# V of a batch in few large loads: pairing attention heads as (i, i+4)

## The chip, the cores and the metric

One core of a Trainium2 chip runs the whole program. The metric is the device time of one execution, in microseconds (us). Engines are written PE (TensorE), DVE (VectorE), ACT (ScalarE), POOL (GpSimd) and SP (SyncE); SPq and POOLq are the instruction queues of SP and POOL in which DMAs are issued.

## What is computed

The reference has two stages. The first is chunked attention over q, k, v of shape (4 batches, 8 heads, 768 positions, 64): each chunk of 32 queries looks at its own keys, 16 keys to the left, 8 to the right, and 8 memory keys of its head.

```python
for c in range(S // 32):
    l_start, r_end = max(0, 32 * c - 16), min(S, 32 * c + 32 + 8)
    k_full = concat(mem_k, k[:, :, l_start:r_end])      # v_full likewise
    scores = q[:, :, 32 * c:32 * c + 32] @ k_full.T / sqrt(64)
    out[:, :, 32 * c:32 * c + 32] = softmax(scores) @ v_full
```

The second stage treats the result as x of shape (4, 768, 512): a dot product with `w_gate` scores each position, the 128 best positions of each batch go through relu(xe @ w1) @ w2, weighted by the sigmoid of their score, and are added to x.

## The kernel before

The work goes by pairs of heads: 16 pairs n, four (pr = 0 to 3) for each batch b. Heads 2*pr and 2*pr+1 form a pair; one lies on partitions 0 to 63 and the other on 64 to 127. The 768 positions of a head are cut into 8 windows (NG) of 96 queries, three chunks each, and a window needs 120 keys.

V lies in one of two buffers (`vbufs`, float32, one for even and one for odd batches) with 128 partitions: 64 for each head of a pair, in four groups of 16 (15 rows of two keys each, and one row of memory values in the 16th). A window reaches 16 keys ahead of its queries, so window 0 begins before the sequence and window 7 ends after it. `load_v` therefore has three sorts of loads for each head and group: windows 1 to 6 (line 91, one load for each pair), window 0 without its first two rows (line 93), and window 7 without its last row (line 95). A fourth sort (line 98) brings the memory values. All are issued on SP. The rows that no load writes are set to zero once, at the start (lines 123 and 124).

`load_qk` issues q and k on POOL (line 81) with a cast to float16. For batch 0 the order is pair 0, pair 1, pairs 2 and 3.

In the loop over n (line 481) an iteration runs, in the order of every engine's program: the scores of pair n+1, first half (PE line 250, exponentials on ACT line 255, called `es`); the transposes of k of pair n+2 (PE line 203, copied by DVE line 220 to `kw`, memory keys filled in by POOL line 227); the values of pair n, first half (PE line 276); `cast_v(n+2)` (ACT line 234, V to float16 in `vc`, one of four slots); the scores' second half; the transposes of q of pair n+3 (ACT line 211 copies them to `qT`); the values' second half; `normalise` (DVE lines 283 and 284, writes x of the batch). Before the loop stand the transposes of pairs 0 and 1, `cast_v(0)`, the scores of pair 0, and `cast_v(1)`.

The second stage of batch b-1 is spread over the iterations of batch b as `hook` steps: dot products (DVE, tile `junk`, line 319), rows (PE 329), comparisons (DVE 353), counts, selection, gather (PE 390), two layers (PE 415 and 424), and a scattered addition into the output (POOL, line 428). `m_store` (SP, lines 305 and 306) writes x of batch b-1 to the output at the start of batch b; the scattered addition waits for that store, and the next store for the addition. The loads of batch b+2 are issued in the iteration with pr == 2 of batch b. After the loop the last batch's second stage runs alone.

The order on each engine is the order in which the program is written (a manual schedule): nothing is moved by a planner, and an instruction that waits holds up all that stand behind it on its engine.

Of the kernel before, what the change touches and what calls it, by code (L numbers as in the profile page):

```python
# [8 lines left out]
FP = mybir.dt.float32  # L9
# [17 lines left out]
def kernel(  # L27
# [13 lines left out]
    nc = tc.nc  # L41
# [37 lines left out]
    def load_qk(b, src, dst, p0, n):  # L79
        h0 = 2 * p0  # L80
        nc.gpsimd.dma_start(out=dst[:, h0:h0 + 2 * n, :],
                            in_=_dap(src, (b * H + h0) * HD, [[512, 96], [HD, 2 * n], [1, 512]]))

    def load_v(b, p0, n):
        t = vbufs[b % 2]
        for h in range(2):
            for jj in range(4):
                o = 64 * h + 16 * jj
                base = (b * H + 2 * p0 + h) * HD + 2 * jj * D
                for i in range(n):  # L90
                    nc.sync.dma_start(out=t[o:o + 15, p0 + i, 1:7, :],  # L91
                                      in_=_dap(v, base + 2 * i * HD + 80 * D, [[8 * D, 15], [96 * D, 6], [1, 128]]))
                nc.sync.dma_start(out=t[o + 2:o + 15, p0:p0 + n, 0, :],  # L93
                                  in_=_dap(v, base, [[8 * D, 13], [2 * HD, n], [1, 128]]))
                nc.sync.dma_start(out=t[o:o + 14, p0:p0 + n, 7, :],  # L95
                                  in_=_dap(v, base + 656 * D, [[8 * D, 14], [2 * HD, n], [1, 128]]))
            for i in range(n):
                nc.sync.dma_start(out=t[64 * h + 15:64 * h + 64:16, p0 + i, :, :],  # L98
                                  in_=_dap(mem_v, (b * H + 2 * (p0 + i) + h) * n_mem * D,
                                           [[2 * D, 4], [0, NG], [1, 128]]))  # L100
# [3 lines left out]
    load_qk(0, q, q16s[0], 0, 1)  # L104
    load_qk(0, k, k16s[0], 0, 1)
# [8 lines left out]
    for p0, n in ((1, 1), (2, 2)):  # L114
        load_qk(0, q, q16s[0], p0, n)
        load_qk(0, k, k16s[0], p0, n)
# [5 lines left out]
    for t in vbufs:  # L122
        nc.vector.memset(t[:, :, 0, :], 0.0)
        nc.vector.memset(t[:, :, 7, :], 0.0)
    for p0 in range(NP):
        load_v(0, p0, 1)
# [19 lines left out]
    ones8 = cst.tile([128, NG], F16, tag="ones8")  # L146
# [12 lines left out]
    def mem_keys():  # L159
        p_mk = pmm.tile([128, NPR, n_mem], F16, tag="pm", name="p_mk")  # L160
        for pr in range(NPR):
            nc.tensor.transpose(out=p_mk[:, pr, :], in_=memk16[:, 2 * pr:2 * pr + 2, :],
                                identity=ident16[0:n_mem, 0:n_mem])
        nc.vector.tensor_copy(out=memkT, in_=p_mk.rearrange("p n (j s) -> p n s j", s=2))
# [149 lines left out]
    def m_dot(b, bls, c0=0, c1=Dm, dst=None):  # L314
        m, x = mods[b], xs[b]
        dst = m.scr if dst is None else dst
        for bl in bls:
            junk = mod.tile([128, Dm], FP, tag="junk", name="junk")
            nc.vector.scalar_tensor_tensor(out=junk[:, c0:c1], in0=x[:, bl, c0:c1], scalar=1.0, in1=wgb[:, c0:c1],  # L319
                                           op0=ALU.mult, op1=ALU.mult, accum_out=dst[:, bl:bl + 1])  # L320

    def m_x16(b, lo, hi, c0=0, c1=Dm):
        nc.vector.tensor_copy(out=mods[b].x16[:, lo:hi, c0:c1], in_=xs[b][:, lo:hi, c0:c1])  # L323
# [157 lines left out]
    for n in range(NPR):  # L481
# [24 lines left out]
        if pr == 2 and b + 2 < B:  # L506
            alloc_batch(b + 2)
            for p0 in (0, 2):
                load_qk(b + 2, q, q16s[b + 2], p0, 2)
                load_qk(b + 2, k, k16s[b + 2], p0, 2)  # L510
                load_v(b + 2, p0, 2)
# [9 lines left out]
    m_dot(b, range(NB), 384, 512, scrB)  # L521
# [6 lines left out]
    m_x16(b, 0, NB, 384, 512)  # L528
# [42 lines left out]
```

## Time and profile before

| | us |
|---|---|
| three runs, median (lowest to highest) | 244.46 (241.13 to 245.14) |
| profiled execution, time | 242.47 |
| profiled execution, span of its instructions | 240.8 |

The span runs from the first instruction to the last; the profiled execution's own time is 1.67 us longer. Busy time within the span was 119.7 us on PE, 83.8 us on DVE, 75.3 us on ACT and 30.7 us on POOL.

### The profile page before, as it was taken

The page shows a single profiled execution, that of the slowest core. Times are in us where ns is not written, and L with a number is a line of the kernel's source. Part 1 is how long each engine was busy: PE and PEld are TensorE (multiplying, and loading weights), DVE is VectorE, ACT ScalarE, POOL GpSimd, SP SyncE. Part 2 cuts the span into 40 slices and gives each one's busy share as a digit, 9 for nine tenths or more (in the row PEclk, how much of TensorE's full clock was granted, in tenths as well). Part 3 has the DMA queues.
Part 4 walks back from the last instruction along what each step waited for, and adds up shares of the span by engine and source line. Part 5 has one row for each costly group of instructions (what it writes and reads, how often), then busy time and mean ns, then how long its engine had stood idle before and what let it go on. Part 6 is the DMA issues. An engine that isn't in the chain of part 4 may idle for free.

```text
span 240.8 us, 5533 instructions
## 1 busy us (share of the span) xinstructions
PE 119.7 (50%) x2264; PEld 98.8 (41%) x2264; DVE 83.8 (35%) x255; ACT 75.3 (31%) x152; POOL 30.7 (13%) x55
## 2 busy tenths in 40 slices
PE   0360801025260079179609920997950478574670
PEld 0350701025250068168608710887740367453540
DVE  6110110011120019348201634673370497548410
ACT  0123203060600282383046450727615252001010
POOL 7254000000050001002200003000000300002011
PEclk9999999999999999999955975557985556677587
DMA  6979994111379222221992275422218380004703
GB/s 93 167 118 206 212 209 87 44 43 44 97 124 209 71 63 58 60 57 54 174 177 55 62 210 130 98 56 72 56 49 264 45 241 26 0 3 87 218 0 44
DMA packets 32681, 24.58 MB, mean 102 GB/s; under 512 B 5264, under 2 KB 28432, under 8 KB 32656
## 3 DMA queue, kind: packets, MB, share of 16 engines
q0 software_dynamic: 9104, 9.47, 25.4%
q1 hardware_dynamic: 23552, 14.76, 22.7%
q8 instruction: 17, 0.28, 0.5%
q14 instruction: 8, 0.07, 0.1%
HBM read 25.30 MB, written 7.34 MB: 136 GB/s over the span
## 4 chain that ended last, share of the span: by engine, by line
SPq 39%; DMA 28%; DVE 10%; PE 9%; issue 9%; ACT 2%; POOL 1%; POOLq 1%; DVEq 0%; ACTq 0%
DMA v<-in_v_dram 22%; SPq L91 16%; SPq L95 9%; SPq L93 8%; SPq L98 6%; DMA out_dram<-x 6%; DVE junk L319 3%; PE p_m L415 3%; DVE gr L353 2%; PE p_x L276 2%; PE p_m L424 2%; ACT es L255 1%; PE p_s L250 1%; PE p_t L203 1%; DVE x L284 1%
## 5 line engine op out<-in xcount | busy, mean ns | idle before, releaser
L255 ACT ACTIVATE es<-p_s,maskb 128x256 f16<-128x256 f32 x96 | 38.6, 479 | 28.0 <-PE p_s L250 28.0
L250 PE MATMUL p_s<-qT,kw 64*64 64x96 f16 x512 | 24.7, 262 | 39.3 <-POOL kw L227 22.2
L234 ACT CAST vc<-v 128x1024 f16<-128x1024 f32 x16 | 16.9, 1056 | 86.7 <-DMA v<-in_v_dram 65.3
L220 DVE COPY kw<-p_t 128x512 f16<-128x512 f16 x32 | 12.1, 419 | 74.9 <-PE p_t L203 74.9
L250 PEld LDWEIGHTS <-kw 64*64 64x64 f16 x512 | 19.6, 148 | 43.3 <-POOL kw L227 22.6
L276 PE MATMUL p_x<-vc,es 64*96 64x65 f16 (+1 forms) x768 | 33.4, 242 | 0.0
L203 PE MATMUL p_t<-ident,k 96*64 96x96 f16 x256 | 12.7, 267 | 35.3 <-ACT qT L211 35.3
L276 PEld LDWEIGHTS <-es 64*96 64x96 f16 (+1 forms) x768 | 26.5, 142 | 5.2 <-issue 0.6
L203 PEld LDWEIGHTS <-k 96*64 96x64 f16 x256 | 10.5, 152 | 37.1 <-issue 36.3
L227 POOL COPY kw<-memkT 128x64 f16<-128x64 f16 x16 | 9.0, 564 | 128.0 <-DVE kw L220 88.5
L284 DVE TENSOR_TENSOR x<-p_x,rd 128x768 f32<-128x768 f32 x16 | 15.3, 958 | 14.6 <-DMA out_dram<-x 14.1
L428 POOL DMA_INDIRECT out_dram<-y,idx x4 | 6.7, 1682 | 75.2 <-DMA out_dram<-x 36.7
L319 DVE SCALAR_TENSOR_TENSOR junk<-x,wgb 128x512 f32<-128x512 f32 (+2 forms) x30 | 15.8, 581 | 0.1
L211 ACT COPY qT<-p_t 128x768 f16<-128x768 f16 x16 | 12.9, 809 | 2.7 <-PE p_t L203 2.7
L353 DVE TENSOR_SCALAR gr<-brow,scr 128x768 f16<-128x768 f32 x24 | 13.4, 617 | 0.1
L203 PE MATMUL p_t<-ident,q 96*64 96x96 f16 x256 | 12.3, 263 | 1.9 <-DVE kw L220 1.8
L283 DVE RECIPROCAL rd<-p_x 128x12 f32<-128x12 f32 x16 | 3.7, 230 | 26.5 <-PE p_x L276 26.5
L415 PEld LDWEIGHTS <-w_sb 128*128 128x128 f16 x128 | 10.4, 123 | 3.9 <-DVE gate L405 3.0
L203 PEld LDWEIGHTS <-q 96*64 96x64 f16 x256 | 10.1, 149 | 3.4 <-issue 2.1
L415 PE MATMUL p_m<-xeT,w_sb 128*128 128x128 f16 x96 | 8.9, 265 | 2.9 <-DVE gate L405 2.9
L390 PEld LDWEIGHTS <-x 128*128 128x128 f16 x96 | 9.3, 138 | 1.3 <-DVE sel L382 0.7
L323 DVE CAST x<-x 128x1024 f16<-128x1024 f32 (+2 forms) x11 | 8.4, 783 | 0.0
(89 smaller groups left out, 101.8 us busy)
## 6 DMA issues: line engine op xcount, KB each, us to landing
v<-in_v_dram SPq DMA_DIRECT2D x128, 45.0 KB
out_dram<-x SPq DMA_DIRECT2D x4, 1152.0 KB
q<-in_q_dram POOLq DMA_DIRECT2D x7, 384.0 KB, 7.2
k<-in_k_dram POOLq DMA_DIRECT2D x7, 384.0 KB, 8.6
w_sb<-in_moe_w_dram POOLq DMA_DIRECT2D x2, 1024.0 KB, 16.0
out_dram<-x SPq DMA_DIRECT2D x4, 384.0 KB
v<-in_v_dram SPq DMA_DIRECT2D x48, 13.0 KB
v<-in_v_dram SPq DMA_DIRECT2D x48, 14.0 KB
```

The lines of the kernel that those rows point to most:

```text
L91: nc.sync.dma_start(out=t[o:o + 15, p0 + i, 1:7, :], in_=_dap(v, base + 2 * i * HD + 80 * D, [[8 * D, 15], [96 * D, 6], [1, 128]]))
L93: nc.sync.dma_start(out=t[o + 2:o + 15, p0:p0 + n, 0, :], in_=_dap(v, base, [[8 * D, 13], [2 * HD, n], [1, 128]]))
L95: nc.sync.dma_start(out=t[o:o + 14, p0:p0 + n, 7, :], in_=_dap(v, base + 656 * D, [[8 * D, 14], [2 * HD, n], [1, 128]]))
L203: nc.tensor.transpose(out=p_t[64 * h:64 * h + 64, j, 2:98], in_=src[b][:, 2 * pr + h, 64 * j:64 * j + 64], identity=ident16[0:96, 0:96])
L234: nc.scalar.copy(out=vcs[n % SLOTS][:, :, :, 0:64], in_=vbufs[b % 2][:, pr, :, :].rearrange("p g (s d) -> p g s d", d=D))
L250: nc.tensor.matmul(out=p_s[o:o + 64, s, 96 * gi:96 * gi + 96], lhsT=kw[o:o + 64, g, s, :], rhs=qf[o:o + 64, 96 * g:96 * g + 96], start=Tru ...
L255: nc.scalar.activation(out=es[:, :, :, 32 * c:32 * c + 32], in_=pv[:, :, :, 32 * c:32 * c + 32], func=AF.Exp, bias=maskb[:, c:c + 1], scal ...
L276: nc.tensor.matmul(out=p_x[r0:r1, h, c0:c0 + 65], lhsT=es[o:o + 64, s, gi, q0:q1], rhs=vc[o:o + 64, GROUPS[half][gi], s, :], start=(s == 0 ...
L284: nc.vector.tensor_tensor(out=xs[b][:, :, 128 * pr:128 * pr + 128].rearrange("p g (h d) -> p h g d", d=D), in0=pv[:, :, :, 0:64], in1=rd.t ...
L319: nc.vector.scalar_tensor_tensor(out=junk[:, c0:c1], in0=x[:, bl, c0:c1], scalar=1.0, in1=wgb[:, c0:c1], op0=ALU.mult, op1=ALU.mult, accum ...
L353: nc.vector.tensor_scalar(out=m.gr[:, bl, :], in0=m.brow, scalar1=m.scr[:, bl:bl + 1], scalar2=None, op0=ALU.is_lt)
L415: nc.tensor.matmul(out=p_h[:, 0, 128 * fi:128 * fi + 128], lhsT=w1_sb[:, dch, f0:f0 + 128], rhs=m.xeT[:, dch, :], start=(dch == 0), stop=( ...
```

## The change

Pairs are now (i, i+4). The lower half of the partitions holds heads 0 to 3 of a batch and the upper half heads 4 to 7. Since a head's 768 positions are exactly eight windows of 96, window 0 of head h+1 stands 96 positions after window 7 of head h, and one load with a step of 96 positions covers all 32 windows of four heads on 15 partitions. A batch then has 8 such loads and 8 of memory values. Windows 0 and 7 now also bring keys of the neighbouring head; `cast_v` multiplies these two windows by a column of zeros and ones (`ones8`) on DVE, while ACT casts windows 1 to 6. Only the very first and the very last head of V, whose neighbour lies outside the tensor, keep separate loads (four each). Batch 0 is loaded as pair 0 and then pairs 1 to 3; the upper half of pair 0 is issued on ACT.

q and k follow: batch 0 loads heads 0 and 4 together, then heads 1 to 3 and 5 to 7 (q, k, q, k); later batches load heads 0 to 3 and 4 to 7. The output columns of `normalise`, the partial dot products and the partial float16 copy for the last batch take the new order of heads.

```diff
-    def load_v(b, p0, n):
-        t = vbufs[b % 2]
-        for h in range(2):
+    def load_v(b, p0, n, engines=(nc.sync, nc.sync)):
+        t = vbufs[b % 2].rearrange("p n g d -> p (n g) d")
+        for hh in range(2):
+            eng = engines[hh]
+            h = 4 * hh + p0
+            lo = 1 if (b, h) == (0, 0) else 0
+            hi = NG * n - 1 if (b, h + n) == (B - 1, H) else NG * n
             for jj in range(4):
-                o = 64 * h + 16 * jj
-                base = (b * H + 2 * p0 + h) * HD + 2 * jj * D
-                for i in range(n):
-                    nc.sync.dma_start(out=t[o:o + 15, p0 + i, 1:7, :],
-                                      in_=_dap(v, base + 2 * i * HD + 80 * D, [[8 * D, 15], [96 * D, 6], [1, 128]]))
-                nc.sync.dma_start(out=t[o + 2:o + 15, p0:p0 + n, 0, :], ...
-                nc.sync.dma_start(out=t[o:o + 14, p0:p0 + n, 7, :], ...
+                o = 64 * hh + 16 * jj
+                base = (b * H + h) * HD + (2 * jj - 16) * D
+                u = NG * p0
+                eng.dma_start(out=t[o:o + 15, u + lo:u + hi, :],
+                              in_=_dap(v, base + 96 * D * lo, [[8 * D, 15], [96 * D, hi - lo], [1, 128]]))
+                if lo:
+                    eng.dma_start(out=t[o + 2:o + 15, u, :], in_=_dap(v, base + 16 * D, [[8 * D, 13], [1, 128]]))
+                if hi < NG * n:
+                    eng.dma_start(out=t[o:o + 14, u + hi, :], in_=_dap(v, base + 96 * D * hi, [[8 * D, 14], [1, 128]]))
             for i in range(n):
-                nc.sync.dma_start(out=t[64 * h + 15:64 * h + 64:16, p0 + i, :, :], ...
+                eng.dma_start(out=t[64 * hh + 15:64 * hh + 64:16, NG * (p0 + i):NG * (p0 + i + 1), :],
+                              in_=_dap(mem_v, (b * H + h + i) * n_mem * D, [[2 * D, 4], [0, NG], [1, 128]]))
...
-    load_qk(0, q, q16s[0], 0, 1)
-    load_qk(0, k, k16s[0], 0, 1)
+    load_qk(0, q, q16s[0], 0, 2, 4)
+    load_qk(0, k, k16s[0], 0, 2, 4)
...
-    for p0, n in ((1, 1), (2, 2)):
-        load_qk(0, q, q16s[0], p0, n)
-        load_qk(0, k, k16s[0], p0, n)
+    for h0 in (1, 5):
+        load_qk(0, q, q16s[0], h0, 3)
+        load_qk(0, k, k16s[0], h0, 3)
...
-    for p0 in range(NP):
-        load_v(0, p0, 1)
+    load_v(0, 0, 1, (nc.sync, nc.scalar))
+    load_v(0, 1, 3)
...
         for pr in range(NPR):
-            nc.tensor.transpose(out=p_mk[:, pr, :], in_=memk16[:, 2 * pr:2 * pr + 2, :], ...
+            b, i = divmod(pr, NP)
+            for hh in range(2):
+                nc.tensor.transpose(out=p_mk[64 * hh:64 * hh + 64, pr, :], in_=memk16[:, b * H + 4 * hh + i, :], ...
...
-        nc.scalar.copy(out=vcs[n % SLOTS][:, :, :, 0:64],
-                       in_=vbufs[b % 2][:, pr, :, :].rearrange("p g (s d) -> p g s d", d=D))
+        vc, vt = vcs[n % SLOTS], vbufs[b % 2]
+        nc.scalar.copy(out=vc[:, 1:7, :, 0:64], in_=vt[:, pr, 1:7, :].rearrange("p g (s d) -> p g s d", d=D))
+        for g in (0, NG - 1):
+            nc.vector.tensor_scalar(out=vc[:, g, :, 0:64], in0=vt[:, pr, g, :].rearrange("p (s d) -> p s d", d=D),
+                                    scalar1=ones8[:, g:g + 1], scalar2=None, op0=ALU.mult)
...
-    for p0 in (0, 2):
-        load_qk(1, q, q16s[1], p0, 2)
-        load_qk(1, k, k16s[1], p0, 2)
-        load_v(1, p0, 2)
+    for h0 in (0, 4):
+        load_qk(1, q, q16s[1], h0, 4)
+        load_qk(1, k, k16s[1], h0, 4)
+    load_v(1, 0, NP)
```

The loads of batches 2 and 3 change like those of batch 1. Of the four memsets on the V buffers two small ones are left.

## Rows read from the trace of the kernel before

**Rows 1.** The page's first part: span and number of instructions.

```profile
span 240.8 us, 5533 instructions
```

**Rows 2.** The page's fourth part: chain that ended last, by engine, then line.

```profile
SPq 39%; DMA 28%; DVE 10%; PE 9%; issue 9%; ACT 2%; POOL 1%; POOLq 1%; DVEq 0%; ACTq 0%
```

**Rows 3.** Waits over the span: us in total, times, longest.

```profile
POOL out_dram L428 <- DMA out_dram<-x: 36.7, 2, 18.5
```

**Rows 4.** Tile v: ns min/median/max, first and last start; who waited for it.

```profile
L91 SPq DMA_DIRECT2D v<-in_v_dram x128: 323/398/2093, 0.8 to 176.2; - x128
L93 SPq DMA_DIRECT2D v<-in_v_dram x80: 306/374/1371, 1.7 to 177.5; - x80
...
L98 SPq DMA_DIRECT2D v<-in_mem_v_dram x32: 522/544/654, 7.4 to 179.3; - x32
...
  ACT vc L234: 86.7, 10
```

**Rows 5.** SP's queue in order of time: start us, us, line.

```profile
49.18 0.39 SPq L91 DMA_DIRECT2D v<-in_v_dram  x1
49.61 0.37 SPq L93 DMA_DIRECT2D v<-in_v_dram  x1
...
139.52 0.41 SPq L305 DMA_DIRECT2D out_dram<-x  x1
```

**Rows 6.** ACT in order of time; in brackets the idle time before, releaser.

```profile
25.03 0.83 ACT L211 COPY qT<-p_t 128x768 f16<-128x768 f16 x1
...
82.92 1.05 ACT L234 CAST vc<-v 128x1024 f16<-128x1024 f32 x1 [17.26 <-DMA v<-in_v_dram]
...
85.63 1.23 ACT L255 ACTIVATE es<-p_s,maskb 128x256 f16<-128x256 f32 x3
...
91.22 1.20 ACT L255 ACTIVATE es<-p_s,maskb 128x256 f16<-128x256 f32 x3 [0.73 <-PE p_s L250]
```

**Rows 7.** DMA queues, 0 to 40 us: packets, MB, share of 16 engines.

```profile
q0 software_dynamic: 5328, 5.28, 82.8%
```

**Rows 8.** DMA queues, 124.5 to 125 us.

```profile
q1 hardware_dynamic: 191, 0.08, 60.3%
```

**Rows 9.** DMA queues, 24 to 28 us.

```profile
q1 hardware_dynamic: 239, 0.10, 13.6%
```

**Rows 10.** DVE in order of time, second stages of batches 0 and 2.

```profile
91.64 0.69 DVE L319 SCALAR_TENSOR_TENSOR junk<-x,wgb 128x512 f32<-128x512 f32 x1
...
97.15 1.29 DVE L323 CAST x<-x 128x1024 f16<-128x1024 f32 x2
105.27 0.76 DVE L220 COPY kw<-p_t 128x512 f16<-128x512 f16 x2 [6.84 <-PE p_t L203]
...
174.63 0.68 DVE L319 SCALAR_TENSOR_TENSOR junk<-x,wgb 128x512 f32<-128x512 f32 x1
...
187.16 0.96 DVE L284 TENSOR_TENSOR x<-p_x,rd 128x768 f32<-128x768 f32 x1 [7.97 <-DMA out_dram<-x]
...
192.57 0.76 DVE L220 COPY kw<-p_t 128x512 f16<-128x512 f16 x2 [2.99 <-PE p_t L203]
...
213.81 0.96 DVE L284 TENSOR_TENSOR x<-p_x,rd 128x768 f32<-128x768 f32 x1
```

**Rows 11.** PE in order of time: the gathers of batches 0 and 1.

```profile
115.29 2.63 PE L390 MATMUL p_m<-sel,x 128*128 128x128 f16 x24
...
162.47 2.74 PE L390 MATMUL p_m<-sel,x 128*128 128x128 f16 x24
```

**Rows 12.** Groups by line and shape: busy us, mean ns of one | idle before.

```profile
L382 DVE TENSOR_SCALAR sel<-iota,slot 128x128 f16<-128x128 f16 x24 | 4.3, 256 | 0.1
...
L319 DVE SCALAR_TENSOR_TENSOR junk<-x,wgb 128x128 f32<-128x128 f32 x6 | 1.3, 287 | 0.0
```

**Rows 13.** Windows of 2 us: busy by engine, PEclk, DMA share, GB/s.

```profile
154.00:156.00 2.00, 2.00 (x48) 1.68 (x46) 2.00 (x4) 1.78 (x4) 0.17 (x1) 0.50 0.29 83
174.00:176.00 2.00, 1.98 (x72) 1.71 (x69) 2.00 (x6) 1.21 (x3) 0.00 (x0) 1.00 0.23 66
```

More of the change, by code (lines that the diff above doesn't have):

```diff
@@ L77, in alloc_batch, with load_qk @@
         k16s[b] = ld.tile([96, H, 512], F16, tag="k16", name=f"k16_{b}")
[L79 to L82, printed above, removed]
-    def load_v(b, p0, n):
-        t = vbufs[b % 2]
-        for h in range(2):
-            for jj in range(4):
-                o = 64 * h + 16 * jj
-                base = (b * H + 2 * p0 + h) * HD + 2 * jj * D
-                for i in range(n):
-                    nc.sync.dma_start(out=t[o:o + 15, p0 + i, 1:7, :],
-                                      in_=_dap(v, base + 2 * i * HD + 80 * D, [[8 * D, 15], [96 * D, 6], [1, 128]]))
[L93 to L96, printed above, removed]
+    def load_qk(b, src, dst, h0, n, step=1):
+        nc.gpsimd.dma_start(out=dst[:, h0:h0 + step * (n - 1) + 1:step, :],
+                            in_=_dap(src, (b * H + h0) * HD, [[512, 96], [step * HD, n], [1, 512]]))
@@ L121 @@
     nc.vector.memset(pads[:, :, 49:50], 0.0)
-    for t in vbufs:
-        nc.vector.memset(t[:, :, 0, :], 0.0)
-        nc.vector.memset(t[:, :, 7, :], 0.0)
-    for p0 in range(NP):
-        load_v(0, p0, 1)
+    for pr, g in ((0, 0), (NP - 1, NG - 1)):
+        nc.vector.memset(vbufs[0 if pr == 0 else 1][:, pr, g, :], 0.0)
+    load_v(0, 0, 1, (nc.sync, nc.scalar))
+    load_v(0, 1, 3)
     wgb = cst.tile([128, Dm], FP, tag="wgb")
@@ L143 @@
     nc.vector.tensor_scalar(out=maskb, in0=maskb, scalar1=1.0, scalar2=-MASKED, op0=ALU.subtract, op1=ALU.mult)
-    ones8 = cst.tile([128, NG], F16, tag="ones8")
+    ones8 = cst.tile([128, NG], FP, tag="ones8")
     nc.vector.memset(ones8, 1.0)
@@ L161, in mem_keys @@
         for pr in range(NPR):
-            nc.tensor.transpose(out=p_mk[:, pr, :], in_=memk16[:, 2 * pr:2 * pr + 2, :],
-                                identity=ident16[0:n_mem, 0:n_mem])
+            b, i = divmod(pr, NP)
+            for hh in range(2):
+                nc.tensor.transpose(out=p_mk[64 * hh:64 * hh + 64, pr, :], in_=memk16[:, b * H + 4 * hh + i, :],
+                                    identity=ident16[0:n_mem, 0:n_mem])
         nc.vector.tensor_copy(out=memkT, in_=p_mk.rearrange("p n (j s) -> p n s j", s=2))
@@ L284, in normalise @@
         nc.vector.tensor_tensor(
-            out=xs[b][:, :, 128 * pr:128 * pr + 128].rearrange("p g (h d) -> p h g d", d=D),
+            out=xs[b].rearrange("p g (h n d) -> p n h g d", n=NP, d=D)[:, pr],
             in0=pv[:, :, :, 0:64], in1=rd.to_broadcast([128, 2, NB, D]), op=ALU.mult)
@@ L312, in m_alloc, with m_dot @@
         m.brow = mod.tile([128, S], FP, tag="brow", name="brow")
-    def m_dot(b, bls, c0=0, c1=Dm, dst=None):
+    def m_dot(b, bls, pr0=0, pr1=NP, dst=None):
         m, x = mods[b], xs[b]
@@ L317, in m_dot, with m_x16 @@
         for bl in bls:
[L318 to L323, printed above, removed]
+            junk = mod.tile([128, 2, Dm // 2], FP, tag="junk", name="junk")
+            o, i, w = (t.rearrange("p (h c) -> p h c", h=2)[:, :, D * pr0:D * pr1] if pr1 - pr0 < NP else t
+                       for t in (junk.rearrange("p h c -> p (h c)"), x[:, bl, :], wgb))
+            nc.vector.scalar_tensor_tensor(out=o, in0=i, scalar=1.0, in1=w, op0=ALU.mult, op1=ALU.mult,
+                                           accum_out=dst[:, bl:bl + 1])
+    def m_x16(b, lo, hi, pr0=0, pr1=NP):
+        o, i = mods[b].x16[:, lo:hi, :], xs[b][:, lo:hi, :]
+        if pr1 - pr0 < NP:
+            o, i = (t.rearrange("p g (h c) -> p g h c", h=2)[:, :, :, D * pr0:D * pr1] for t in (o, i))
+        nc.vector.tensor_copy(out=o, in_=i)
     def m_row(b, lo, hi, eng=None):
@@ L507 @@
             alloc_batch(b + 2)
[L508 to L511, printed above, removed]
+            for h0 in (0, 4):
+                load_qk(b + 2, q, q16s[b + 2], h0, 4)
+                load_qk(b + 2, k, k16s[b + 2], h0, 4)
+            load_v(b + 2, 0, NP)
         if n == NPR - 2:
             m_alloc(LAST)
-            m_dot(LAST, range(NB), 0, 384, scrA)
-            m_x16(LAST, 0, NB, 0, 384)
+            m_dot(LAST, range(NB), 0, 3, scrA)
+            m_x16(LAST, 0, NB, 0, 3)
     b = LAST
@@ L520 @@
     scrB = mod.tile([128, NB], FP, tag="scrB", name="scrB")
-    m_dot(b, range(NB), 384, 512, scrB)
+    m_dot(b, range(NB), 3, 4, scrB)
     nc.vector.tensor_tensor(out=mods[b].scr, in0=scrA, in1=scrB, op=ALU.add)
@@ L527 @@
     m_gate(b)
-    m_x16(b, 0, NB, 384, 512)
+    m_x16(b, 0, NB, 3, 4)
     m_mask(b)
```

5 lines of the change are left out of this document (1 added, 4 removed).

## The prediction

> **What bounds the kernel now.** I read the page's chain first. It gives 39% of the span to SP's queue and 28% to DMA, and only 21% to the three engines that compute [rows 2]: the end is set by issuing and landing loads. The waits of tile v say which. SP issues 320 of them: 128 on line 91, 80 on line 93, 80 more on line 95 at 0.37 us, 32 on line 98 [rows 4]. By their medians that is 50.9 + 29.9 + 29.6 + 17.4 = 128 us of issuing, spread from 0.8 to 179 us, and the timeline shows them shoulder to shoulder: one of 0.39 us at 49.18, the next at 49.61 [rows 5]. ACT, whose cast needs V, waits 86.7 us for them in ten places [rows 4]; the cast of pair 4 begins at 82.92 after 17.26 us of waiting [rows 6]. The reader is to see one queue as the pacemaker, with no compute engine above half of the span.
>
> The queue does a second harm. The store of batch 0's x stands behind V of batch 2 on SP and is issued at 139.52 [rows 5], though the second stage of that batch began at 91.64 [rows 10]. The scattered addition waits for the store: 36.7 us on POOL in two places [rows 3], and the memory keys queued behind it on POOL, then the scores, come late. DVE waits for x to be stored as well, 7.97 us once [rows 10].
>
> **What the change removes.** By the diff SP issues 23 V loads for batch 0, then 16, 16 and 20: 75, and ACT five. A large load has more rows but is still one instruction. At 0.40 and 0.54 us [rows 4] a whole batch is 8 x 0.40 + 8 x 0.54 = 7.5 us of issuing in place of 29 (32, 16, 16 and 8 of the four sorts) or, for batch 0 (32, 32, 32 and 8), 41. The store of 576 rows takes 0.41 us to issue [rows 5], where a load of 90 rows takes 0.40: the price is by instruction, so I don't scale it by rows. Issuing then no longer paces anything, and the stores leave SP at the start of a batch, as soon as x is ready and the previous addition landed. With the cover gone, a store would matter only if late by the four iterations until its x buffer is written again.
>
> **What is late next: arrival of V of batch 1.** Each batch's V now lands as a whole, not pair by pair. V of batch 0 is 4,096 rows of 512 bytes (128 partitions, 8 windows, 4 pairs), V of batch 1 as many, and they share 16 engines with q, k and the weights. POOL's queue keeps the engines busy 82.8% of the first 40 us, 33.1 us of work [rows 7]. In a burst, SP's rows come at 191 in 0.5 us for 60.3% of 16 engines [rows 8]: 0.603 x 16 x 0.5 / 191 = 25.3 ns of one engine, so both batches cost 8,192 x 25.3 ns / 16 = 12.9 us. Together 46 us, if the engines are never idle. I take 46 us for the cast of pair 4, against 82.92. Bounds: compute cannot be there before 39. The last copy before the cast of pair 1 ends at 25.86, its exponentials start one cast later at 26.9, an iteration took 91.22 - 85.63 = 5.6 us [rows 6], two of them and 1.1 us of exponentials give 39.2. At the other end SP's rows came at only 239 in 4 us, 60 per us, beside a busy POOL queue [rows 9]; 40 us of that bring 2,400, and the other 5,800 at the burst's 382 per us take 15 us more: 55.
>
> **The rest, from rows, with its stalls taken out.** (a) From the cast of pair 4 to the first dot product of batch 0's second stage: 91.64 - 82.92 = 8.7 us. (b) One batch with a second stage in it: from that dot product to the end of the float16 copy, 98.44 - 91.64 = 6.8; then a stall on V until 105.27, left out; from there to the end of the gather, 117.92 - 105.27 = 12.65; and, from the other batch, from the end of its gather to the next first dot product, 174.63 - 165.20 = 9.4 [rows 10, 11]. Sum 28.9 us, twice. (c) From the last batch's first dot product to its last x: 214.77 - 174.63 = 40.1, less the stalls of 7.97 (store) and 2.99 (memory keys behind the addition) [rows 10] = 29.2. (d) From there to the end of the span, 240.8 - 214.77 = 26.0 [rows 1, 10]: the last second stage alone, which the change leaves as it is.
>
> **What is added.** DVE casts two windows for each pair, 32 instructions of 128 x 128. No row shows this operation; the nearest are 256 ns (float16 input) and 287 ns (two float32 inputs) [rows 12]. Eight for a batch are at most 2.3 us; they cost nothing where PE sets the pace. In the first two iterations of a batch DVE is the busy one (6.8 us without a gap, above), in the others PE is: I take half of the lower price, 1.0 us a batch and 0.5 in (c), whose last two iterations have none. ACT's cast loses a quarter of its 1.05 us [rows 6], so the ends are 1 us gained and 2.3 lost for a batch; I book no gain, since ACT mostly waits for PE (0.73 us at 91.22) [rows 6].
>
> The casts on DVE are also a new wait: behind the cast of pair 1 stand the copies of k for pair 2, and PE's next transposes and scores wait for those. The lower bound of 39 already runs iteration 0 whole after that cast, so its price is inside it. From batch 2 on, V is in the queue a batch ahead. Sixteen more small transposes and 2.2 us of issues on ACT lie where both wait for the first loads: nothing, about 3 us if that cover went. Pair 1's keys now come in the last two of four loads; a few us, hidden while 39 is below 46. Two memsets fewer gain nothing for the same reason.
>
> **The sum.** 46 + 8.7 + 2 x 29.9 + 29.7 + 26.0 = 170.2 us of span; with the profiled execution's 1.7 us outside it, 172. That execution took 242.47, 0.8% below the median of the three runs, so I give 172 against 244.46. By the bounds of V (39 to 55) and of the casts it is 163 to 184.
>
> **Rivals.** *The clock helps.* At a granted clock of 0.50 PE issued 48 matmuls in 2 us, at 1.00, after a gather and a layer, 72 [rows 13]. It fell after stalls on V. If it now stays up from batch 1's layers on, the 12.65 us of (b) shrink to 8.4 once, and as much goes in (c): 8 us less, 164, and 157 with V at 39. Against it: DVE's first two iterations leave PE gaps in every batch.
>
> *Large loads land more slowly.* The burst of 382 rows per us was of several small loads, bound for different groups of partitions. In the new order eight large ones, each on a group of 15, follow one another in the same queue. If a single group takes half the burst's rate, 191 per us, 5,800 rows after the busy first 40 us take 30 us, V of batch 1 is there at 70, and the time is 196. No row has one group alone. [...]
>
> *Slower than before.* The place is the same queue, the mechanism that a deep ring of large loads gets no more than the 60 rows per us seen beside POOL's queue [rows 9], even later. The end is then the landing of batch 3's V plus 8.7 + 29.7 + 26.0 = 64.4 us. It passes 240.8 when 16,384 rows need more than 176 us, below 93 per us, and just there the change would do nothing; at 60 it gives 339 us. Against it stands the burst: 60.3% of 16 engines is ten engines at work on such loads.
>
> **Chances.** Forecast (163 to 184) 0.50; clock (157 to 163) 0.12; slower landing (184 to 198) 0.18; below 157, 0.04; between 198 and the old time 0.10, where a wait that I don't see would lie; no change 0.02; slower 0.04. The range 157 to 198 leaves out 0.20. The runs before lie within 1.7%, so 2% is what can be told from no change: faster 0.94, same 0.02, slower 0.04.
>
> **What would show it.** Some 80 V loads, not 320, and no run of issues on SP; the cast of pair 4 near 46 us and the only long wait for V there or before; first dot products of the second stages some 30 us apart; the first store issued at that dot product, not 40 us later; 26 us after the last x. It would be wrong if V's casts still wait in batches 2 and 3, if DVE fills whole iterations past the second of a batch, or if the first V of batch 0 comes later than 39 us.

## The result and the profile after

The changed kernel takes 193.72 us, median of four executions (193.39 to 196.31), beside 244.0 us for the kernel before (241.13 to 245.14). The ratio is 0.797, 95% interval 0.788 to 0.806: faster. The forecast was 172 us, so the sign is right, and the time is 22 us later. It lies above the forecast's own band (163 to 184) and inside the stated range of 157 to 198 only because that range takes in the band of the rival *Large loads land more slowly* (184 to 198, chance 0.18). The profiled execution took 193.39 us.

The page's span and chain, which answer to [rows 1] and [rows 2]:

```profile
span 191.7 us, 5338 instructions
...
DMA 37%; DVE 25%; PE 22%; issue 6%; SPq 5%; ACT 1%; POOLq 1%; ACTq 0%; DVEq 0%
```

SP's queue has fallen from 39% of the chain to 5%, but DMA has risen from 28% to 37%: issuing no longer ends last, landing does. Tile v, as in [rows 4]:

```profile
L96 SPq DMA_DIRECT2D v<-in_v_dram x36: 323/440/4757, 0.8 to 104.9; - x36
...
L103 SPq DMA_DIRECT2D v<-in_mem_v_dram x31: 521/527/5666, 6.8 to 113.2; - x31
...
L96 ACTq DMA_DIRECT2D v<-in_v_dram x4: 330/394/661, 1.3 to 3.7; - x4
...
  ACT vc L240: 35.6, 2
```

With two times four edge loads that is the 75 issues on SP and, with one of mem_v, the five on ACT that were counted, and ACT waits for V in two places instead of ten. Which two, its queue shows in order of time (as [rows 6]):

```profile
20.46 0.84 ACT L240 CAST vc<-v 128x768 f16<-128x768 f32 x1
32.90 0.83 ACT L240 CAST vc<-v 128x768 f16<-128x768 f32 x1 [8.71 <-DMA v<-in_mem_v_dram]
...
70.95 0.84 ACT L240 CAST vc<-v 128x768 f16<-128x768 f32 x1 [26.94 <-DMA v<-in_v_dram]
74.53 0.88 ACT L240 CAST vc<-v 128x768 f16<-128x768 f32 x1
```

The third of these is the cast of pair 4, the first of batch 1. It was forecast for 46 us and came at 70.95, after 26.94 us of waiting. No later cast waits for V. What follows can be read off DVE (as [rows 10]): three first dot products, and the last x.

```profile
79.46 0.69 DVE L329 SCALAR_TENSOR_TENSOR junk<-x,wgb 128x512 f32<-128x512 f32 x1
...
108.67 0.68 DVE L329 SCALAR_TENSOR_TENSOR junk<-x,wgb 128x512 f32<-128x512 f32 x1
...
137.31 0.68 DVE L329 SCALAR_TENSOR_TENSOR junk<-x,wgb 128x512 f32<-128x512 f32 x1
...
165.19 0.96 DVE L292 TENSOR_TENSOR x<-p_x,rd 128x768 f32<-128x768 f32 x1
```

So 70.95 + 8.5 + 29.2 + 28.6 + 28.8 + 25.6 = 191.7. The whole error lies in the first term. SP's queue (as [rows 5]) shows what the queue does meanwhile:

```profile
25.01 12.06 SPq L96 DMA_DIRECT2D v<-in_v_dram  x4
45.51 12.41 SPq L96 DMA_DIRECT2D v<-in_v_dram  x4
...
75.50 6.40 SPq L96 DMA_DIRECT2D v<-in_v_dram  x4
86.21 0.35 SPq L313 DMA_DIRECT2D out_dram<-x  x1
```

Four large loads of V of batch 1 take SP 12 us, not 4 x 0.40, while earlier loads are still landing. All 16 issues for that batch took SP 37 us. The store of batch 0 leaves at 86.21, not 139.52.

The DMA queues (packets, MB, share of 16 engines), first over 0 to 70 us, then SP's queue over 20 to 60, over 60 to 70 and over 16 to 20 us (as [rows 7 to 9]):

```profile
q0 software_dynamic: 6928, 6.85, 62.4%
q1 hardware_dynamic: 9077, 4.62, 46.5%
q10 hardware_dynamic: 576, 0.26, 1.6%
...
q1 hardware_dynamic: 4870, 2.59, 41.8%
...
q1 hardware_dynamic: 1890, 0.93, 69.6%
...
q1 hardware_dynamic: 911, 0.45, 117.9%
```

Three readings. In 0 to 70 us a packet of SP's queue took 0.465 x 16 x 70 / 9,077 = 57 ns of an engine, not the 25.3 ns of [rows 8]. SP's queue landed 4,870 / 40 = 122 rows per us beside a busy POOL queue, and 189 per us when POOL's queue was nearly empty. And the shares can't be read as time that an engine is lost to others: over 0 to 70 us they add up to 110%, and SP's queue alone shows 117.9% over 16 to 20 us, so the times of packets overlap. The 57 ns is how long a packet took there, and such prices don't add up to a landing time.

### The profile page after: what moved, and what is told of

The parts are those of the page before. It is cut to its first block, busy times and chain, and to the rows that moved or that the text cites. A ratio compares the mean times of both kernels' runs of the same rounds, so it can differ in the third digit from the quotient of the medians.

```text
span 191.7 us, 5338 instructions
## 1 busy us (share of the span) xinstructions
PE 116.6 (61%) x2280; PEld 95.5 (50%) x2280; DVE 89.0 (46%) x285; ACT 72.4 (38%) x152; POOL 31.1 (16%) x55
## 4 chain that ended last, share of the span: by engine, by line
DMA 37%; DVE 25%; PE 22%; issue 6%; SPq 5%; ACT 1%; POOLq 1%; ACTq 0%; DVEq 0%
DMA v<-in_v_dram 25%; DMA v<-in_mem_v_dram 7%; DVE junk L329 6%; PE p_x L284 6%; DVE gr L366 5%; SPq L96 4%; PE p_m L428 4%; DMA out_dram<-x 3%; DVE x L292 3%; PE p_m L437 3%; PE p_t L208 3%; PE p_m L403 3%; DVE x L336 3%; DMA out_dram<-y,idx 3%; PE p_s L258 3%
## 5 line engine op out<-in xcount | busy, mean ns | idle before, releaser
L284 PE MATMUL p_x<-vc,es 64*96 64x65 f16 (+1 forms) x768 | 32.0, 235 | 1.3 <-DVE x L292 0.7
L208 PE MATMUL p_t<-ident,k 96*64 96x96 f16 x256 | 11.9, 253 | 31.3 <-ACT qT L216 28.4
L284 PEld LDWEIGHTS <-es 64*96 64x96 f16 (+1 forms) x768 | 25.5, 136 | 6.2 <-issue 1.7
L242 DVE TENSOR_SCALAR vc<-v,ones 128x128 f16<-128x128 f32 x32 | 8.8, 343 | 39.8 <-DMA v<-in_v_dram 26.2
L240 ACT CAST vc<-v 128x768 f16<-128x768 f32 x16 | 13.5, 845 | 35.6 <-DMA v<-in_v_dram 26.9
L208 PEld LDWEIGHTS <-k 96*64 96x64 f16 x256 | 9.5, 141 | 32.9 <-issue 27.4
L258 PE MATMUL p_s<-qT,kw 64*64 64x96 f16 x512 | 23.4, 253 | 0.5 <-ACT es L263 0.5
L258 PEld LDWEIGHTS <-kw 64*64 64x64 f16 x512 | 18.3, 141 | 4.3 <-issue 2.0
L225 DVE COPY kw<-p_t 128x512 f16<-128x512 f16 x32 | 12.1, 419 | 11.4 <-PE p_t L208 10.5
L208 PEld LDWEIGHTS <-q 96*64 96x64 f16 x256 | 10.3, 145 | 12.1 <-issue 10.6
L428 PEld LDWEIGHTS <-w_sb 128*128 128x128 f16 x128 | 8.8, 110 | 3.2 <-DVE gate L418 2.4
L376 PEld LDWEIGHTS <-gr 128*128 128x128 f16 x144 | 5.4, 105 | 8.2 <-DVE gr L366 7.8
```

The lines of the kernel that those rows point to most:

```text
L208: nc.tensor.transpose(out=p_t[64 * h:64 * h + 64, j, 2:98], in_=src[b][:, pr + 4 * h, 64 * j:64 * j + 64], identity=ident16[0:96, 0:96])
L225: nc.vector.tensor_copy(out=kw[:, :, s, :].rearrange("p g (j t) -> p g j t", t=16), in_=_sap(p_t, 100 * s, [[12, NG], [200, 4], [1, 16]]))
L240: nc.scalar.copy(out=vc[:, 1:7, :, 0:64], in_=vt[:, pr, 1:7, :].rearrange("p g (s d) -> p g s d", d=D))
L258: nc.tensor.matmul(out=p_s[o:o + 64, s, 96 * gi:96 * gi + 96], lhsT=kw[o:o + 64, g, s, :], rhs=qf[o:o + 64, 96 * g:96 * g + 96], start=Tru ...
L284: nc.tensor.matmul(out=p_x[r0:r1, h, c0:c0 + 65], lhsT=es[o:o + 64, s, gi, q0:q1], rhs=vc[o:o + 64, GROUPS[half][gi], s, :], start=(s == 0 ...
L428: nc.tensor.matmul(out=p_h[:, 0, 128 * fi:128 * fi + 128], lhsT=w1_sb[:, dch, f0:f0 + 128], rhs=m.xeT[:, dch, :], start=(dch == 0), stop=( ...
```

## Experiments

The question is why V of batch 1 lands at 71 us. Theories, by letter in the expectations: G, a large load goes to one group of 15 neighbouring partitions, and such a group takes rows slowly whoever issues them; R, a row has its price wherever it goes, and SP's queue only shares the engines; Q, the weights on POOL's queue take V's turn. One thing that none of them says came out later: how much of V has to be there before pair 4 can start.

**m1_rates: V loads alone.** The kernel only loads V of a batch five times over (the attention and the second stage are left out), with a small DVE copy after each part.

`part(engine, hh, jj, i, n)` issues the load of half hh and group jj for n pairs from pair i on:

```diff
(1) part(nc.sync, hh, jj, 0, 4)                        8 loads of 32 windows
(2) part((nc.sync, nc.scalar)[hh], hh, jj, 0, 4)       upper half on ACT
(3) for i, hh, jj: part(nc.sync, hh, jj, i, 1)         32 loads of 8 windows, groups in turn
(4) for hh, jj, i: part(nc.sync, hh, jj, i, 1)         the same, one group four times
(5) one load of 128 partitions, 32 rows each
```

Expected:

> Only loads of V of batch 1 (no attention, no second stage, the output is not computed), five ways one after the other, each started when the one before has landed: (1) the eight large loads of 32 windows on SP; (2) the same, upper half issued on ACT; (3) 32 loads of 8 windows on SP, the partition group changing with each load; (4) the same 32 loads, four in a row on the same group; (5) the same number of 512-byte rows on all 128 partitions in one load. Theory G (a load's own group of 15 partitions admits about 220 rows per us, as the changed kernel showed at 16 to 20 us): (1) 17 to 19 us, (2) 9 to 11, (3) 13 to 14 (32 issues of 0.4 us) , (4) 17 to 19, (5) 8 to 10. Rival R (512-byte rows cost the same wherever they land, 81 ns of an engine): all five 16 to 19 us. Rival I (SP waits for an earlier load to land before it can issue another): (3) and (4) alike and slower than (1).

DVE in order of time; the wait ahead of each copy is the landing time of the part before it:

```profile
29.36 0.19 DVE L77 COPY junk<-t 128x32 f32<-128x32 f32 x1 [24.00 <-DMA t<-in_v_dram]
47.85 0.19 DVE L77 COPY junk<-t 128x32 f32<-128x32 f32 x1 [18.30 <-DMA t<-in_v_dram]
64.80 0.19 DVE L77 COPY junk<-t 128x32 f32<-128x32 f32 x1 [16.76 <-DMA t<-in_v_dram]
88.81 0.19 DVE L77 COPY junk<-t 128x32 f32<-128x32 f32 x1 [23.81 <-DMA t<-in_v_dram]
99.12 0.19 DVE L77 COPY junk<-t 128x32 f32<-128x32 f32 x1 [10.12 <-DMA t<-in_v_dram]
```

Parts (1) to (4) are the same 8 x 15 x 32 = 3,840 rows. Large loads land at 3,840 / 24.0 = 160 rows per us, and so do small ones that stay with a group (4). Small ones that go round the groups (3) come at 229, about as fast as SP issues them (32 in 16.8 us), and 4,096 rows over all partitions (5) at 405, near the 382 of [rows 8]. With nothing else in the queues, R falls and the direction of G holds: (3) and (4) are the same loads in another order, so it is not the size of the load but the partitions in flight together. G's sizes don't hold: it gave 17 to 19 us for (1) and (4) and 9 to 11 for (2), the upper half on a second queue, which took 18.3. And (5) also reads neighbouring rows of memory, which the others don't, so the 405 isn't shown to come from the partitions alone.

**m2_groups: which groups go together.** Again loads alone (the rest is left out): one load of 15 partitions x 128 rows on SP, then with a second one on ACT that begins 32, 16 and 64 partitions further, then the kernel's rows in loads of 60 neighbouring partitions, on one queue and on two.

```diff
-for hh, jj, i: part(nc.sync, hh, jj, i, 1)
+part(nc.sync, 0, 15, 128)
+part(nc.sync, 0, 15, 128); part(nc.scalar, 32, 15, 128)     # then 16, then 64 for 32
+part(nc.sync, 0, 60, 32);  part(nc.sync, 64, 60, 32)        # then the second on nc.scalar
```

Expected:

> Only loads of 512-byte rows of V (no attention, no second stage, the output is not computed), six parts, each started when the one before has landed: (1) one load of 15 partitions (0 to 14) x 128 rows on SP; (2) the same and, on ACT, one to partitions 32 to 46; (3) the same and, on ACT, one to 16 to 30; (4) the same and, on ACT, one to 64 to 78; (5) two loads of 60 neighbouring partitions x 32 rows, 0 to 59 and 64 to 123, both on SP; (6) the same, the second on ACT. [...] Rival E (any second queue doubles the rate, since the limit is that engines work through one load in step): (2), (3) and (4) alike, 12 to 15. Rival A (the engines are simply full): (2), (3), (4) alike, 22 to 25.

```profile
32.47 0.30 DVE L77 COPY junk<-t 128x128 f32<-128x128 f32 x1 [14.21 <-DMA t<-in_v_dram]
56.48 0.30 DVE L77 COPY junk<-t 128x128 f32<-128x128 f32 x1 [23.71 <-DMA t<-in_v_dram]
75.11 0.30 DVE L77 COPY junk<-t 128x128 f32<-128x128 f32 x1 [18.33 <-DMA t<-in_v_dram]
94.11 0.30 DVE L77 COPY junk<-t 128x128 f32<-128x128 f32 x1 [18.70 <-DMA t<-in_v_dram]
107.73 0.30 DVE L77 COPY junk<-t 128x128 f32<-128x128 f32 x1 [13.32 <-DMA t<-in_v_dram]
118.51 0.30 DVE L77 COPY junk<-t 128x128 f32<-128x128 f32 x1 [10.48 <-DMA t<-in_v_dram]
```

One group alone takes 1,920 / 14.21 = 135 rows per us. A second one costs 9.5 us more if it lies 32 partitions away, and 4.1 or 4.5 if it lies 16 or 64 away. So groups 16 or 64 apart don't land free of each other either, and neither rival's picture of three like times fits. Loads of 60 partitions, 3,840 rows, come at 288 rows per us on one queue and 366 on two; they too read neighbouring rows of memory. What sets 32 partitions apart from 16 and 64 no run here shows.

**e1_weights_late: the weights issued after iteration 3.**

```diff
     late_constants()
-    load_w()
...
+        if n == 3:
+            load_w()
```

Expected:

> The two weight loads of POOL are issued after iteration 3, once V of batch 1 has landed; all else as in the changed kernel. Theory G (the partition group is the limit whatever POOL does): V of batch 1 still lands near 70 us, time 190 to 194. Rival Q (V is late because POOL's loads take the 16 engines): the weights' 22 us beside V go, the cast of pair 4 starts near 60 us, time 180 to 186.

193.01 us (ratio 0.793, 0.784 to 0.803). The cast of pair 4 comes at 66.58, 4.4 us earlier, and the casts of pairs 8 and 12 then wait 4.91 and 1.18 us for mem_v. Q is real and small here, and it is given back.

**e3_two_queues: the upper half of V of batch 0, pairs 1 to 3, issued by ACT.** The loads stay large.

```diff
-    load_v(0, 1, 3)
+    load_v(0, 1, 3, (nc.sync, nc.scalar))
```

Expected:

> The upper half of the second load of batch 0 (pairs 1 to 3) is issued on ACT, the rest as in the changed kernel. Theory G: the two halves land side by side, the cast of pair 1 starts at 25 to 28 us in place of 32.9, the cast of pair 4 some 5 us sooner, time 187 to 190. Rival Q: less than 2 us of change, 192 to 195. Rival I: ACT itself waits at its issues for landings, its first copies come later, time 194 to 200.

183.25 us (0.754, 0.748 to 0.760), below every range that was given. The queues over 14 to 30 us:

```profile
q1 hardware_dynamic: 2960, 1.65, 75.6%
q10 hardware_dynamic: 1296, 0.63, 19.8%
q0 software_dynamic: 122, 0.11, 5.0%
```

ACT in order of time, the cast of pair 4:

```profile
57.27 0.83 ACT L240 CAST vc<-v 128x768 f16<-128x768 f32 x1 [9.86 <-DMA v<-in_mem_v_dram]
```

Two queues landed 4,256 packets in these 16 us; the changed kernel landed 2,775. The 1,481 more, at the 122 per us that follow, are 12.1 us, and pair 4 is 13.7 us earlier. But POOL's queue moved only 0.11 MB in the same stretch (0.80 before the edit): ACT's first copy stood 20.0 us behind its own issues, so what comes after it came later, the first load of batch 1's q too (24.1 us, not 19.1). How much of the 13.7 us is the second queue and how much the absence of POOL's traffic stays open.

**e2_split8: one load for each pair and group (8 windows), pair by pair.**

```diff
-        for hh in range(2):                 # 32 windows in a load
-            for jj in range(4):
+        for i in range(n):
+            for hh in range(2):             # 8 windows of pair p0+i in a load
+                for jj in range(4):
```

Expected:

> Each large load of V is split by pair of heads into loads of 8 windows, in the order pair, half, group, so that the partition group changes with every load and pairs land one after the other; 40 loads on SP per batch in place of 16. Theory G: rows come faster and pair 4 needs only a quarter of the batch, the cast of pair 4 starts at 45 to 55 us, time 168 to 180. Rival Q: V still gets only its share beside POOL's loads, the cast of pair 4 comes sooner by the three quarters that it does not wait for, but the later pairs wait in turn: 185 to 194. Rival I (issue limited by landings): slower than 194.

185.55 us (0.764, 0.758 to 0.769). The cast of pair 4 comes at 47.47, close to the forecast's 46 and 23.5 us earlier; that is in G's range, while the time is at the edge of Q's. ACT in order of time, pairs 3 and 4:

```profile
40.15 0.83 ACT L240 CAST vc<-v 128x768 f16<-128x768 f32 x1 [8.21 <-DMA v<-in_v_dram]
47.47 0.83 ACT L240 CAST vc<-v 128x768 f16<-128x768 f32 x1 [3.59 <-DMA v<-in_v_dram]
```

It would be easy to put all of that down to G. The queues over 0 to 47 us say otherwise. The changed kernel:

```profile
q1 hardware_dynamic: 5551, 2.88, 46.1%
q10 hardware_dynamic: 576, 0.26, 2.4%
```

This one:

```profile
q1 hardware_dynamic: 5770, 2.80, 26.8%
q10 hardware_dynamic: 576, 0.26, 2.2%
```

Nearly the same number of rows has landed: 6,127 and 6,346. (A packet is cheaper now, 0.268 x 16 x 47 / 5,770 = 35 ns, but small loads cost SP about 0.5 us for 120 rows, and POOL's queue is as busy as before.) By the count, V of batch 0 and at least a quarter of batch 1 are there at 47 us in either kernel. In this one the quarter is all of pair 4; with large loads it is a part of each of four pairs, and none of them started before 70.95. This share of the delay is the merging itself: pair 4 waits there for loads that bring all four pairs.

The gain at the start is 20 us at the first dot product (59.3), and a good half of it is lost: the next ones follow after 30.7 and 35.6 us. V of batch 2 is 40 issues again, and the store stands behind them (issued at 91.57).

**e4_cast_act: ACT casts all eight windows** (the zeroing of the keys outside a sequence is left out).

```diff
-        nc.scalar.copy(out=vc[:, 1:7, :, 0:64], in_=vt[:, pr, 1:7, :]...)
-        for g in (0, NG - 1): nc.vector.tensor_scalar(...)
+        nc.scalar.copy(out=vc[:, :, :, 0:64], in_=vt[:, pr, :, :]...)
```

Expected:

> ACT casts all eight windows of V again and DVE's 32 casts are gone; the zeroing of the keys outside a head's sequence is left out, so those keys' values are wrong. All loads as in the changed kernel. As predicted (half of DVE's casts lie on the path, 1.0 us a batch): 190 to 192. If all of them do (0.29 us each, 9 us): 183 to 186. If none: 193 to 195. The cast of pair 4 stays at 70 us in all three.

192.49 us (0.791, 0.784 to 0.797). The first dot products are 28.8 and 27.7 us apart instead of 29.2 and 28.6: by these two profiles the casts on DVE cost 0.4 to 0.9 us a batch. Neither the times nor the profiles settle it: the intervals of the two kernels overlap, and the granted clock was 0.92 by the mean in this profile and 0.89 in the other.

**e5_sixty: keys ordered so that a half of V is one load of 60 neighbouring partitions.**

```diff
-                eng.dma_start(out=t[o:o + 15, ...], in_=_dap(v, ..., [[8 * D, 15], ...]))   # four groups
+            eng.dma_start(out=t[o:o + 60, ...], in_=_dap(v, ..., [[2 * D, 60], ...]))
...
-            nc.vector.tensor_copy(out=kw[:, :, s, :].rearrange("p g (j t) -> p g j t", t=16), ...
+            nc.vector.tensor_copy(out=kw[:, :, s, :].rearrange("p g (t j) -> p g j t", j=4), ...
```

Expected:

> The keys of a window are put on the partitions in the order row, group in place of group, row; the rows of a half are then 60 neighbouring partitions 512 bytes apart in memory, and one load brings them for all windows: 2 large loads and 8 small of memory values per batch. Mask, copies of k and memory keys follow the order. Theory G (a group of 15 partitions is the limit): a batch's V lands in 12 us instead of 24 when nothing else loads, the cast of pair 4 starts at 42 to 52 us, time 168 to 178. Rival Q (POOL's loads take the engines): cast of pair 4 at 62 to 70, time 186 to 193.

188.63 us (0.776, 0.769 to 0.782). Pair 4 is cast at 54.10, nearer to G's range than to Q's, and the time is in Q's. Two new costs are seen. The copies of k, whose output now goes in steps of four elements, take three times as long (groups by line; busy us, mean ns):

```profile
L225 DVE COPY kw<-p_t 128x512 f16<-128x512 f16 x32 | 38.5, 1303 | 14.5 <-PE p_t L208 14.5
```

SP stands for long at its mem_v issues, whose price for the time wasn't traced (its queue in order of time):

```profile
27.27 15.89 SPq L102 DMA_DIRECT2D v<-in_mem_v_dram  x4
```

After the change these copies take 419 ns by the mean. There are 8 in a batch, so DVE has 8 x 0.88 = 7.1 us more for each, and the first dot products are 32.6 and 33.1 us apart instead of 29.

**e6_spread: e2, with V of batches 2 and 3 issued pair by pair over four iterations.** The store of batch 0 then stands behind 20 issues, not 40.

```diff
-            load_v(b + 2, 0, NP)
+        if n >= 2 and n + 6 < NPR:
+            load_v((n + 6) // NP, (n + 6) % NP, 1)
```

Expected:

> Loads of 8 windows as in the run with one load for each pair and group, and the V loads of batches 2 and 3 issued pair by pair over four iterations instead of all at once, so that the store of batch 0 stands behind 20 V issues on SP and not 40. In the run before it the first dot of batch 0 began at 59.3 us, but the next ones followed after 30.7 and 35.6 us, with POOL held for 15.1 us by the store. If that late store is what gave the gain back: first dots near 59, 89, 118 and 147 us and the last 26 us, so 173 + 2 = 175 us (range 172 to 179). If the second period was long because V of batch 2 itself comes late, the spread loads come no earlier, the period stays over 34 us and the time at 183 to 187 us.

181.73 us (0.750, 0.745 to 0.756), 3.8 less than e2 and not the 10 expected. The store leaves at 77.27 instead of 91.57, and the second period is 31.8 us instead of 35.6. Of the 2.8 us that it still has over 29, pair 10 has its part: its loads now stand behind the store, and it is cast 12.1 us after pair 9 (6.9 in the changed kernel). The first period is 32.0 us, 1.3 more than in e2, which I haven't traced.

**e7_spread_weights: e6, with the weights after iteration 3** (the edit of e1).

Expected:

> The same, and the weights issued after iteration 3. With large loads this brought the cast of pair 4 4.4 us earlier and cost it back in waits of pairs 8 and 12. If V of batch 1 is now limited by how fast SP issues (about 0.5 us for each of 40 loads), the cast of pair 4 stays within 2 us of 47.5 and the time within 2 us of the run without this edit. If the weights take its bandwidth, the cast of pair 4 and of pair 5 come some 4 us earlier and the time is 3 to 5 us lower.

181.71 us (0.753, 0.747 to 0.760). The cast of pair 4 moves from 47.32 to 39.33, twice what was expected of Q, close to where the forecast let compute hold it (39.2); pairs 5 and 6 then wait 5.32 and 8.22 us, and the time is that of e6. (The profiled executions of this kernel and the next are not the median ones: 178.29 us here, the shortest of four, and 178.02 there, the longest.)

**e8_spread_act: e6, with the upper half of V of batch 0, pairs 1 to 3, on ACT** (the edit of e3).

Expected:

> The spread loads, and the upper half of V of batch 0, pairs 1 to 3, issued by ScalarE. It takes 15 of the issues ahead of V of batch 1 away from SP, 8 us. If SP's issuing is the bound the cast of pair 4 comes near 41 us (PE's own work then holds it) and the time is 4 to 6 us lower, 169 to 171 us; if ScalarE stands behind its own issues, as with the large loads, where its first copy waited 20 us, the start is later by up to 6 us and the time is the same or higher, 175 to 179 us.

177.63 us (0.731, 0.724 to 0.739), the best version: its interval lies below that of the change. The cast of pair 4 is at 42.98, near the 41 expected, and the time still 7 us above the expected, since the dot products are 31.8 and 35.7 us apart. (It lies in the range of the other branch, a late ACT, but not by that way: ACT's first cast does come 7.4 us later than in e6, and pair 4 doesn't.) For the second of these periods, SP's queue shows a long stand:

```profile
77.88 11.24 SPq L97 DMA_DIRECT2D v<-in_v_dram  x4
```

ACT, at the cast of pair 10:

```profile
93.65 0.83 ACT L240 CAST vc<-v 128x768 f16<-128x768 f32 x1 [7.97 <-DMA v<-in_v_dram]
```

Four of the eight loads for pair 10 take 11.24 us behind the store (issued at 72.53), and pair 10 waits 7.97 us.

**e9_store_act and e10_store_act_all: the stores moved to ACT**, with V of batches 2 and 3 spread (e9) or all at once (e10).

```diff
-        nc.sync.dma_start(out=_dap(out, b * S * Dm, ...), in_=x[0:96, :, :])
+        nc.scalar.dma_start(out=_dap(out, b * S * Dm, ...), in_=x[0:96, :, :])
```

Expected of e9:

> The best run so far (loads of 8 windows, spread, the upper half of V of batch 0 issued by ScalarE: first dots at 52.8, 84.6, 120.3 and 151.8 us, so periods of 31.8, 35.7 and 31.5 instead of the 29 of the changed kernel), with the two stores of each batch issued by ScalarE instead of SP. In that run four V issues behind the store took SP 11.24 us and pair 10 then waited 7.97 us for V. If V stands behind the store on SP's queue, the periods fall to 29 to 30 us: dots at 53, 83, 112 and 141, and 141 + 26 + 2 = 169 us (range 166 to 172). If the store and V only share the engines' bandwidth, the periods stay at 31 to 35 us and the time at 175 to 179 us.

Expected of e10:

> The same with V of batches 2 and 3 issued all at once, 40 issues in a row as the run with loads of 8 windows first had it. With the store on another queue nothing of POOL waits behind these issues; if that is all that the spread was for, the time is that of the spread form within 2 us; if the loads crowd out the store's transfer, the scatter comes late and POOL holds mem_k's copies up again: 3 to 8 us more.

A miss: 199.75 us (0.825, 0.820 to 0.829) and 200.57 us (0.827, 0.823 to 0.831), slower than the change itself (and e10 within 1 us of e9, as its first branch had it). POOL of e9 in order of time shows the scattered addition of batch 0:

```profile
93.71 1.87 POOL L441 DMA_INDIRECT out_dram<-y,idx  x1 [5.91 <-DMA v<-in_v_dram]
```

ACT shows what I had overlooked:

```profile
99.46 0.32 ACTq L313 DMA_DIRECT2D out_dram<-x  x1
99.83 0.52 ACTq L314 DMA_DIRECT2D out_dram<-x  x1
100.45 1.20 ACT L263 ACTIVATE es<-p_s,maskb 128x256 f16<-128x256 f32 x3 [9.07 <-issue]
```

The store of batch 1 may not start before the scattered addition of batch 0 has landed (issued at 93.71), and ACT has the exponentials behind it: 9.07 us of idle time here, 8.50 at the next store. SP can afford to stand there; ACT can't.

That isn't the whole loss. The first period is already 40.1 us, against 31.8 in e8, and the store in it, that of batch 0, waits for no addition. ACT at that store and at the next cast of V, pair 6:

```profile
53.26 0.35 ACTq L313 DMA_DIRECT2D out_dram<-x  x1
...
66.67 0.83 ACT L240 CAST vc<-v 128x768 f16<-128x768 f32 x1 [11.20 <-DMA v<-in_v_dram]
```

From 53 to 66 us SP's queue landed 407 packets, and 2,146 in e8, whose store leaves later; the page of e9 has its two highest rates there, 253 and 270 GB/s in the slices from 54 to 64 us. So V is held up by a store on another queue too, by 11.20 us here and 10.66 in e10: its place behind the store in SP's queue, the first branch of e9's expectation, isn't needed for that wait. That the two share the engines, the second branch, fits; which part of the way they share, no run here shows.

## Why the prediction was right in sign and 22 us early

**What bounds the kernel, and what is removed: right, but for the price of an issue.** The V issues are 80 as counted, they end no chain any more, and the wait of POOL on the store, 36.7 us in [rows 3], is gone from the list of waits. The store left 6.8 us after the first dot product and not at it, since SP stood 6.4 us at four V loads and 3.2 at four of memory values; nothing waited for it. "The price is by instruction" did not hold: the 16 issues for batch 1 took SP 37 us where 7.5 were booked.

**(a) to (d), from rows with their stalls taken out: right.** Forecast 8.7, twice 29.9, 29.7 and 26.0; measured 8.5, 29.2 and 28.6, 28.8, 25.6. The pieces of (b) fit too: 7.2, 13.0 and 9.0 us in the first period, against 6.8, 12.65 and 9.4. The DVE casts, booked at 1.0 us a batch, cost 0.4 to 0.9 as far as e4 tells; one takes 288 ns by its median, at the upper of the two prices in [rows 12]. From pair 8 on no cast waits for V, as said. Pair 1 waits 8.71 us, more than the "few us", but under the cover of pair 4's wait.

**The step that failed: "Together 46 us, if the engines are never idle."** Its bounds, 39 and 55, failed with it; V of batch 1 was there at 70.95.
- The price of a row. 25.3 ns of an engine was read where several groups were in flight [rows 8]. With large loads it was 57 ns, by which 8,192 rows are 29 us of 16 engines, not 12.9. Alone, loads to one group after another land at 160 rows per us and not at 382 (m1, m2).
- The sum itself. It adds shares of 16 engines as if packets took turns, and they overlap (110% over 0 to 70 us).
- The other traffic. POOL's queue shows 0.624 x 70 = 43.7 us of the engines before V of batch 1 was there, not 33.1: q and k of batch 2 are issued by POOL at 45.5 to 48.2 us, ahead of the last of V. Holding the weights back gave 4.4 us (e1).
- What pair 4 waits for. The forecast says that V "lands as a whole, not pair by pair", and gives that no price of its own. It has one. In e2 as many rows were there at 47 us, and pair 4 started then.

These aren't independent shares of 25 us: the edits e1, e3 and e2, each alone, moved pair 4 by 4.4, 13.7 and 23.5 us, and part of each was taken back later.

**The rivals.** *Large loads land more slowly*, with a chance of 0.18, is what happened in time and, in part, in cause: V at 70 and 196 us forecast, 70.95 and 193.7 measured. It had the right place (one group of 15 partitions in a queue), but its sum came out partly by luck. That a single group takes half of the burst's rate, 191 rows per us, was a supposition: one group alone took 135 (m2), eight large loads one after another 160 (m1). The rival had 2,400 rows landed at 40 us, then 191 per us; in the profile some 5,400 had landed by 40 us, and the rest came at 143 per us, slower as POOL's queue stayed busy until 60 (122 beside it, 189 when it was nearly empty).

*The clock helps* is not borne out, and its price had no ground. It let the 12.65 us of (b) shrink with a higher clock, but PE had run that stretch (105 to 118 us) at a granted clock of 1.00 in the kernel before, and from 104 to 116 us it issued 255 matmuls in 12 us, 42 in 2 us, no more than the 48 at 0.50. So 48 against 72 is a matter of which matmuls, too. Windows (as [rows 13]), first of the kernel before, then of the changed one:

```profile
104.00:116.00 12.00, 12.00 (x255) 10.22 (x254) 9.14 (x28) 5.12 (x12) 3.57 (x6) 1.00 0.28 57
...
99.00:121.00 22.00, 18.72 (x460) 14.82 (x457) 15.67 (x44) 15.93 (x34) 3.28 (x4) 0.97 1.02 165
122.00:129.00 7.00, 6.86 (x115) 6.09 (x117) 4.57 (x17) 1.92 (x5) 0.46 (x1) 0.50 0.34 107
```

In the changed kernel the granted clock was 0.97 from 99 to 121 us and 0.50 from 122 to 129, and both periods stayed at 29 us. *Slower than before* needed under 93 rows per us; in the crowded stretch there were 122.

What the experiments add: with pair 4 as early as 39 to 47 us, the next batches become the bound. In e2, e6, e7 and e8 the first two periods are 30.7 to 37.7 us instead of 29. V of batches 1 to 3 and the stores are in transit there together; in e8 7.97 us is a wait for V seen behind a store, e9 shows such a wait with the store on another queue, and the rest wasn't traced. So a first term of 43 to 47 us gave 177.6 to 185.6 us in these versions, not 172.

## What to carry to other kernels

When small loads are merged, the price of a row has to be read from loads that go to the same partitions in the same order, beside the traffic that will be there; a burst to many groups (382 rows per us in [rows 8]) is a bound, not an estimate: large loads to one group after another came at 160 alone (m1) and at 122 beside POOL's queue. Merging also merges completion: ask how many rows must be there before the first consumer can start (with about as many landed at 47 us, pair 4 started at 47.47 in e2 and at 70.95 in the changed kernel). A transfer that must wait for another one belongs on a queue whose engine has nothing else to do (ACT stood idle for 9.07 and 8.50 us at such stores in e9); another queue alone didn't take a large store out of the way of the loads (11.20 us of waiting for V in e9).

## What was unexpected of the hardware

One group of 15 partitions took 135 rows of 512 bytes per us (m2), 128 partitions 405 (m1): a factor of three at the same row size (the second from neighbouring rows of memory). Two loads to groups 16 or 64 partitions apart, on two queues, took 18.3 and 18.7 us where one took 14.2, and 32 apart 23.7 (m2). A DVE copy of 128 x 512 from float16 to float16 took 1,303 ns with its output in steps of four elements (e5) and 419 ns in the layout before. Four small mem_v loads held SP for 15.89 us in e5, with large loads in the queue ahead of them, for a reason that no run here settles.
